# Two small products of the tensor engine rewritten, and the instruction order searched anew

## The chip, the core and the metric

The kernel runs on one core of a Trainium2 chip. A core has five engines with queues of their own: TensorE (PE, matmuls; PEld stands for its loads of weights), VectorE (DVE), ScalarE (ACT), GpSimd (POOL) and SyncE (SP, which issues most DMAs). The metric is the device time of one execution in microseconds, as the median of several runs: 402.71 us before the change, with single runs from 401.82 to 403.29.

## The reference

Two stages. The first is windowed attention over 8 batches, 8 heads, 576 positions and 64 channels; the second a gated attention of four experts on its output x.

```python
scores = scale * np.matmul(q, k.transpose(0, 1, 3, 2))      # stage 1, per batch and head
mask = (rel >= 0) & (rel < 64)                              # a window of 64 positions
attn = softmax(where(mask, scores, -1e9))
x = attn @ v                                                # heads side by side: 576 x 512
for e in range(4):                                          # stage 2, per batch
    q, k, v = x @ wq[e], x @ wk[e], x @ wv[e]               # 512 -> 64
    a = softmax(causal(scale * q @ k.T))
    out += gate[:, e] * (a @ v @ wo[e])                     # the best 2 of 4 experts by x @ w_gate
```

## The kernel before

Stage 1 works on pairs of heads: 32 pairs, 9 blocks of 64 queries each, in 72 groups. For a group `m` multiplies q and k (L344, fp32, tiles of 64 x 32 of the array), `q` is its softmax on DVE, ACT and POOL, `t` transposes (L414) and `a` multiplies with v (L440, tiles of 64 x 64) and writes x to SBUF as a high and a low fp16 part (L465 on ACT, L467 on DVE).

Before x is split in two fp16 parts it is scaled by a bound per batch: no entry of x is larger than the largest entry of v. Unit `n` (`s1_top`) reduces v of a batch to one maximum per partition, on DVE (L483, L486). Unit `M` (`s1_scale`) makes one number of these 128 and puts it on all partitions: a transpose by PE (L490), a maximum along the row by DVE (L493), a product of a row of ones with that number by PE (L495), and a scale and its reciprocal by DVE (L498, L499). Unit `N` works out further factors.

Stage 2 takes a batch b and a pair of experts pr at a time. `v`, `k` and `r` are the projections (L592 to L594, three fp16 products high x high, high x low, low x high, on the full array of 128 x 128). The projected q, transposed, has the 64 channels of one expert on partitions 0 to 63 and those of the other on 64 to 127. It is copied out of PSUM as a high part by ACT (L675) and a low one by DVE (L683; in batch 0 by POOL, L681) into `QT`; a projection is done in two halves of 320 and 256 queries. `x` multiplies q with k (L717, tiles of 64 x 128, one per expert), `y` is the softmax, `u` weighs it, `D` transposes it (by DMA, for the last pair partly by PE, L811), `A` multiplies with v (L843, tiles of 128 x 64), `o` is the output projection.

The first 64 queries of both experts are one unit `x` of their own, `k == 4`: six products of 64 x 64, three per expert, the one expert's result on partitions 0 to 63, the other's on 64 to 127 (L708).

The order of all work is written by hand in the table `ORDER`, a list of units: each name stands for the next step of that unit (up to its next `yield`), and the digits behind a colon name the PSUM banks that the step takes. Each engine runs its instructions in that order. Units `F` only keep PE busy: products of a constant matrix that nobody reads (L892); so do the first ones, whose number per bank is in `FILL` (L222).

Of the kernel before, what the change touches and what calls it, by code (L numbers as in the profile page):

```python
# [42 lines left out]
FILL = "44444444"  # L43

ORDER = (
# [101 lines left out]
)  # L147


@with_exitstack  # L150
def window_attention_moe_attention(ctx: ExitStack, tc: tile.TileContext, qT, kT, vW,
# [10 lines left out]
    def bank():  # L162
        return PS[:, banks.pop(0)]
# [844 lines left out]
```

## Time and profile before

| | |
|---|---|
| median of 3 runs | 402.71 us (401.82 to 403.29) |
| the profiled execution | 402.01 us |
| its span, first to last instruction | 400.3 us |
| mean granted clock of TensorE | 0.998 |
| PE busy | 385.6 us, 96% |
| DVE busy | 341.2 us, 85% |
| ACT busy | 330.9 us, 83% |
| POOL busy | 307.7 us, 77% |
| DMA, mean | 178 GB/s |

The rows quoted further down belong to this one profiled execution. A busy PE counts from the start of a matmul to its modelled end, and such records overlap; from one start to the next is what a matmul holds PE for. The idle time behind a bar in a row is the time in which the engine waited before it, with the one that ended it.

### The profile page before, as it was taken

Reading aid. Unit: us, or ns where it says so; the run is one execution under the profiler, and the core shown is the slowest. Engines: PE = TensorE matmul, PEld = TensorE weight load, DVE = VectorE, ACT = ScalarE, POOL = GpSimd, SP = SyncE. Lnnn points to the kernel's source line nnn. Section 1 sums busy time; section 2 is a strip of 40 time slices with the busy share of each in tenths; the row PEclk is TensorE's granted clock in tenths of the full one; section 3 lists DMA queues with packets and bytes.
Section 4 is the critical chain, followed back from the end, with each engine's and each line's share of the span. In section 5 each row is a group of like instructions: output and inputs, shape, how many; then the busy total and the mean of one; then the engine's idle time right before and its main releaser. Section 6 shows DMA issues by size and latency. Waiting matters only on the chain. (4 is left out here: it accounts for less than half of the span.)

```text
span 400.3 us, 18293 instructions
## 1 busy us (share of the span) xinstructions
PE 385.6 (96%) x7288; PEld 289.2 (72%) x7288; DVE 341.2 (85%) x1040; ACT 330.9 (83%) x1163; POOL 307.7 (77%) x686
## 2 busy tenths in 40 slices
PE   8899999999999999999999999999999999999985
PEld 8777777777777776777766866787767767777563
DVE  2898999899889778998898989888999698789872
ACT  2878899989788888898898998988989898876762
POOL 7375757988788888897698987898787986988520
PEclk9999999999999999999999999999999999999999
DMA  7942713699978987899959995799949592798993
GB/s 230 389 155 105 228 25 128 206 177 211 199 156 188 200 143 250 176 220 229 182 122 227 167 182 189 146 278 174 239 99 160 100 168 107 106 172 145 193 214 133
DMA packets 142677, 71.25 MB, mean 178 GB/s; under 512 B 123392, under 2 KB 126720, under 8 KB 142592
## 3 DMA queue, kind: packets, MB, share of 16 engines
q1 hardware_dynamic: 142080, 69.56, 80.1%
q8 instruction: 57, 0.93, 1.0%
q10 hardware_dynamic: 512, 0.52, 0.4%
q14 instruction: 28, 0.23, 0.2%
HBM read 30.94 MB, written 9.44 MB: 101 GB/s over the span
## 5 line engine op out<-in xcount | busy, mean ns | idle before, releaser
L794 POOL TENSOR_TENSOR sp<-p,sp 128x320 f16<-128x320 f32 (+3 forms) x110 | 101.6, 923 | 9.2
L732 ACT ACTIVATE p<-p,r 128x576 f32<-128x576 f32 (+3 forms) x128 | 77.5, 612 | 6.9 <-DVE r L728 5.9
L372 ACT ACTIVATE p<-ps,st 128x64 f32<-128x64 f32 x216 | 65.2, 320 | 10.0 <-POOL st L369 6.8
L783 ACT ACTIVATE sp<-p,r 128x320 f16<-128x320 f32 (+3 forms) x114 | 68.1, 615 | 2.7 <-POOL r L769 2.0
L793 POOL TENSOR_SCALAR p<-p,r 128x320 f32<-128x320 f32 (+3 forms) x110 | 65.0, 591 | 3.5 <-ACT sp L783 2.2
L728 DVE CUSTOM_DVE_ANT_0 p<-ps,causal,sc 128x320 f32<-128x320 f32 (+2 forms) x128 | 63.8, 541 | 4.4 <-PE ps L717 3.7
L397 POOL TENSOR_TENSOR p<-p,st 128x256 f32<-128x256 f32 x72 | 43.5, 613 | 6.4 <-DVE st L393 4.4
L418 DVE TENSOR_TENSOR pt<-ps,tri 128x1024 f32<-128x1024 f32 (+1 forms) x40 | 44.5, 1111 | 4.3 <-PE ps L414 3.2
L372 ACT ACTIVATION_READ_ACCUMULATOR p<-ps,st 128x1 f32 x216 | 45.8, 212 | 0.0
L717 PE MATMUL ps<-kt,qt 64*128 64x320 f16 (+3 forms) x480 | 40.1, 292 | 0.6 <-DVE r L728 0.3
L440 PE MATMUL ps<-pt,vt 64*64 64x128 f32 (+1 forms) x1440 | 39.3, 249 | 0.9 <-DVE xl L467 0.4
L440 PEld LDWEIGHTS ps<-pt,vt 64*64 64x64 f32 x1440 | 34.1, 133 | 8.2 <-DVE r L728 2.2
L843 PE MATMUL ps<-tu,v 128*64 128x64 f16 (+2 forms) x1056 | 39.0, 229 | 0.9 <-DMA tu<-sp 0.4
L843 PEld LDWEIGHTS <-v 128*64 128x64 f16 x1056 | 35.8, 111 | 4.6 <-issue 3.2
L344 PE MATMUL ps<-k,q 64*32 64x96 f32 (+2 forms) x2304 | 37.8, 244 | 0.8 <-issue 0.5
L592 PE MATMUL ps<-xh,wkhi 128*128 128x256 f16 (+1 forms) x128 | 36.7, 287 | 0.9 <-DVE p L379 0.5
L592 PE MATMUL ps<-xh,wqhi 128*128 128x320 f16 (+1 forms) x128 | 36.7, 287 | 0.1
L593 PE MATMUL ps<-xl,wqhi 128*128 128x320 f16 (+1 forms) x128 | 36.6, 286 | 0.0
L594 PE MATMUL ps<-xh,wklo 128*128 128x256 f16 (+1 forms) x128 | 36.6, 286 | 0.0
L594 PE MATMUL ps<-xh,wqlo 128*128 128x320 f16 (+1 forms) x128 | 36.6, 286 | 0.0
L593 PE MATMUL ps<-xl,wkhi 128*128 128x256 f16 (+1 forms) x128 | 36.6, 286 | 0.0
L344 PEld LDWEIGHTS ps<-k,q 64*32 64x32 f32 x2304 | 29.8, 106 | 9.3 <-issue 5.8
(168 smaller groups left out, 1022.7 us busy)
## 6 DMA issues: line engine op xcount, KB each, us to landing
vt<-in_vW_dram SPq DMA_DIRECT2D x16, 576.0 KB, 4.9
q<-in_qT_dram SPq DMA_DIRECT2D x14, 576.0 KB, 5.2
k<-in_kT_dram SPq DMA_DIRECT2D x14, 576.0 KB, 5.9
out_dram<-out SPq DMA_DIRECT2D x29, 256.0 KB, 3.2
tu<-sp SPq DMA_TRANSPOSE x94, 4.2
out_dram<-out SPq DMA_DIRECT2D x10, 128.0 KB, 3.7
q<-in_qT_dram SPq DMA_DIRECT2D x2, 320.0 KB, 7.8
k<-in_kT_dram SPq DMA_DIRECT2D x2, 320.0 KB, 8.1
```

The costliest lines, as they stand in the source:

```text
L344: nc.tensor.matmul(S1[g][o:o + 32, i, c:c + n], lhsT=q_t[r, i % 2, q0:q0 + 32], rhs=k_t[r, i % 2, k0:k0 + n], start=True, stop=True)
L372: nc.scalar.activation(pt[:, i], ps[:, i, 64:128], AF.Exp, bias=st[:, 0, z + i:z + i + 1], scale=0.125, accum_out=st[:, 1, z + i:z + i + 1])
L440: nc.tensor.matmul(to, lhsT=values[d][r, h, b + e - (w == 0)], rhs=rhs, start=(e, h) not in started, stop=s == n - 1, skip_group_check=True)
L592: nc.tensor.matmul(ps, lhsT=ah, rhs=bh, start=first, stop=False)
L593: nc.tensor.matmul(ps, lhsT=ah, rhs=bl, start=False, stop=False)
L594: nc.tensor.matmul(ps, lhsT=al, rhs=bh, start=False, stop=last)
L728: nc.vector.tensor_tensor_reduce(out=dst, in0=src, in1=mask, scale=SC[b][:, 3:4], scalar=above, op0=OP.add, op1=OP.min, accum_out=to)
L732: nc.scalar.activation(p, p, AF.Exp, bias=r2[:, 0, x:x + 1], scale=-1.0, accum_out=r2[:, 1, x:x + 1])
L783: nc.scalar.activation(hi, p, AF.Copy, scale=by)
L793: nc.gpsimd.tensor_scalar(p, p, by, 1.0, op0=OP.mult, op1=OP.mult)
L794: nc.gpsimd.tensor_tensor(lo, p, hi, op=OP.subtract)
L843: nc.tensor.matmul(to, lhsT=V2[b % 2][:, c, a, 2 * pr + h], rhs=rhs, start=n == 0, stop=n == len(work_list) - 1, skip_group_check=True)
```

## The change

The bound of v: POOL multiplies the 128 x 128 identity by the 128 maxima, which gives a diagonal matrix (now the last step of `s1_top`), and one product of a full matrix of ones with that diagonal puts all 128 maxima on every partition; DVE takes the maximum along the columns there. The first product, its bank and the 1 x 1 tile between are gone.

The first 64 queries: their projected q goes to a matrix `Q0` of 128 x 128, expert 0's block in the upper left, expert 1's in the lower right, zeros elsewhere (cleared once). One product on the full array then gives both experts' scores: three products of 128 x 128 by 64 columns in place of six of 64 x 64. To fill `Q0`, the copy of the first half of q becomes three copies, both for the high and the low part: one of 256 queries on all partitions, and two of 64 queries on half of them.

The table ORDER is another one throughout, and the fillers at the start are 5 per bank in place of 4, over the same 512 columns.

```diff
--- before.py
+++ after.py
@@ -40,110 +40,110 @@
-FILL = "44444444"
+FILL = "55555555"
 ORDER = (
-    'f:01234567 p0 p1 c l0 h0 h1 i l2 l1 z p0 Fa0_3:0 m2:7 p1 m0:6 l3 Fa1_4:5 m1:5 q0 h2 d q2 q0 e0 m3:4 q0 q1 w0 q1 '
...
+    'f:01234567 p0 c p1 l0 h0 h1 i l2 Fa0_3:0 m0:7 p0 z l1 p1 m2:6 q0 l3 Fa1_4:5 m3:5 q0 q2 h2 d m1:4 q0 q0 q0 q1 w0 '
...
@@ -203,7 +203,7 @@
     win = const.tile([128, 64], F32, name="win")
     tri = const.tile([128, 2, 64], F32, name="tri")
     above_one = const.tile([128, 128], BF16, name="above_one")
-    one = const.tile([1, 128], F32, name="one")
+    ones = const.tile([128, 128], F32, name="ones")
 
     past = win.bitcast(U32)
 
@@ -226,7 +226,7 @@
                                     channel_multiplier=1, compare_op=OP.is_ge, fill=NEG)
         make_identity(nc, ident)
         nc.gpsimd.memset(above_one, 1.015625)
-        nc.gpsimd.memset(one, 1.0)
+        nc.gpsimd.memset(ones, 1.0)
 
     def tri_constants():
         nc.vector.memset(tri, 1.0)
@@ -476,6 +476,7 @@
             nc.gpsimd.tensor_scalar(XT[b9 & ~1, x][:, :, b9 % 2], last, 1.0, 1.0, op0=OP.mult, op1=OP.mult)
 
     MV = {}
+    MD = {}
 
     def s1_top(b):
         MV[b] = work.tile([128, 3], F32, tag="mv", name=f"mv_{b}")
@@ -484,18 +485,20 @@
                                     axis=AX.X, op=OP.max, apply_absolute_value=True)
             yield
         nc.vector.tensor_tensor(MV[b][:, 2:3], MV[b][:, 0:1], MV[b][:, 1:2], op=OP.max)
+        yield
+        MD[b] = work.tile([128, 128], F32, tag="md", bufs=1, name=f"md_{b}")
+        nc.gpsimd.tensor_scalar(MD[b], ident, MV[b][:, 2:3], 1.0, op0=OP.mult, op1=OP.mult)
 
     def s1_scale(b):
-        ps = bank()
-        nc.tensor.transpose(ps[0:1, 0:128], MV[b][:, 2:3], ident)
-        yield
-        m = work.tile([1, 1], F32, tag="m1", name=f"m1_{b}")
-        nc.vector.tensor_reduce(m, ps[0:1, 0:128], axis=AX.X, op=OP.max)
-        yield
-        nc.tensor.matmul(ps[:, 256:257], lhsT=one, rhs=m, start=True, stop=True)
+
+        ps = bank()[:, 0:128]
+        nc.tensor.matmul(ps, lhsT=ones, rhs=MD[b], start=True, stop=True)
+        yield
+        m = MV[b][:, 0:1]
+        nc.vector.tensor_reduce(m, ps, axis=AX.X, op=OP.max)
         yield
         sc = SC[b] = work.tile([128, 5], F32, tag="sc", bufs=3, name=f"sc_{b}")
-        nc.vector.tensor_scalar(sc[:, 1:2], ps[:, 256:257], 1e-30, 1.0 / UP, op0=OP.max, op1=OP.mult)
+        nc.vector.tensor_scalar(sc[:, 1:2], m, 1e-30, 1.0 / UP, op0=OP.max, op1=OP.mult)
         nc.vector.reciprocal(sc[:, 0:1], sc[:, 1:2])
 
     def s2_scale(b):
@@ -511,6 +514,7 @@
 
     L = [const.tile([128, 5, E], F32, name=f"logits{i}") for i in range(2)]
     QT = [const.tile([128, 2, S], F16, name=f"qt{i}") for i in range(2)]
+    Q0 = [const.tile([128, 2, 2, 64], F16, name=f"q0_{i}") for i in range(2)]
 
     Y8 = [[const.tile([128, 2, 512], F16, name=f"y{b}{i}") for i in range(2)] for b in range(2)]
     Y1 = [const.tile([128, 2, 128], F16, name=f"y2{i}") for i in range(2)]
@@ -571,6 +575,8 @@
         nc.gpsimd.memset(below, 0.0)
         for e in range(1, E):
             nc.gpsimd.memset(below[:, e, 0:e], 1.0)
+        for x in Q0:
+            nc.gpsimd.memset(x, 0.0)
 
     def clear_v2(x):
         nc.gpsimd.memset(V2[x][64:128, 4], 0.0)
@@ -672,25 +678,35 @@
         return ps, c0, n
 
     def parts(b, x, ps, hi, lo):
-        nc.scalar.activation(hi, ps, AF.Copy, scale=1.0 / UP)
+
+        for r, c, to in hi:
+            nc.scalar.activation(to, ps[r, c], AF.Copy, scale=1.0 / UP)
         yield
         if b == 0:
             t = TURN[1][1][:, 320 * x:320 * x + ps.shape[-1]]
             nc.scalar.activation(t, ps, AF.Copy, scale=1.0 / UP)
             yield
-            nc.gpsimd.tensor_tensor(lo, t, hi, op=OP.subtract)
+            for (r, c, to), (_, _, up) in zip(lo, hi):
+                nc.gpsimd.tensor_tensor(to, t[r, c], up, op=OP.subtract)
         else:
-            nc.vector.scalar_tensor_tensor(lo, ps, 1.0 / UP, hi, op0=OP.mult, op1=OP.subtract)
+            for (r, c, to), (_, _, up) in zip(lo, hi):
+                nc.vector.scalar_tensor_tensor(to, ps[r, c], 1.0 / UP, up, op0=OP.mult, op1=OP.subtract)
 
     def s2_k(b, pr, half):
         ps, c0, n = proj(b, "k", pr, half)
         yield
-        yield from parts(b, half, ps, *(KT[pr][:, x, c0:c0 + n] for x in range(2)))
+        yield from parts(b, half, ps, *([(slice(0, 128), slice(0, n), KT[pr][:, x, c0:c0 + n])] for x in range(2)))
 
     def s2_q(b, pr, half):
         ps, c0, n = proj(b, "q", pr, half)
         yield
-        yield from parts(b, 2 + half, ps, *(QT[pr][:, x, c0:c0 + n] for x in range(2)))
+        if half:
+            to = [[(slice(0, 128), slice(0, n), QT[pr][:, x, c0:c0 + n])] for x in range(2)]
+        else:
+            to = [[(slice(0, 128), slice(64, n), QT[pr][:, x, 64:n])] +
+                  [(slice(64 * e, 64 * e + 64), slice(0, 64), Q0[pr][64 * e:64 * e + 64, x, e]) for e in range(2)]
+                  for x in range(2)]
+        yield from parts(b, 2 + half, ps, *to)
 
     SCORES = (((1, 0, 192), (2, 0, 320)), ((3, 0, 448),), ((4, 0, 320),), ((4, 320, 256),))
 
@@ -703,10 +719,8 @@
         if k == 4:
             ps = SB[b, pr, k] = bank()
             for x, (w, m) in enumerate(((0, 0), (0, 1), (1, 0))):
-                for e in range(2):
-                    r = slice(64 * e, 64 * e + 64)
-                    nc.tensor.matmul(ps[r, 0:64], lhsT=QT[pr][r, w, 0:64], rhs=KT[pr][r, m, 0:64],
-                                     start=x == 0, stop=x == 2)
+                nc.tensor.matmul(ps[:, 0:64], lhsT=Q0[pr][:, w].rearrange("r e q -> r (e q)"), rhs=KT[pr][:, m, 0:64],
+                                 start=x == 0, stop=x == 2)
             return
         ps = SB[b, pr, k] = [bank() for e in range(2)]
         for i, key, n in SCORES[k]:
```

On PE, the bound of v of batch 0 stood like this before. L490 is the transpose of the maxima (`mv`), L495 the product with ones, L414 transposes of stage 1, L344 scores of stage 1, L892 a filler:

```order
L344 MATMUL ps<-k_182,q_181 32x96 x4
L344 MATMUL ps<-k_178,q_177 32x96 x4
L344 MATMUL ps<-k_182,q_181 32x96 x4
L490 MATMUL ps<-ident,mv_347 1x128
L414 MATMUL ps<-ident,p_2_323 128x64 x4
L414 MATMUL ps<-ident,p_3_362 128x64 x4
L892 MATMUL ps<-ident 128x128 x3
L495 MATMUL ps<-m_0_478,one 128x1
L344 MATMUL ps<-k_178,q_177 32x96 x4
```

and stands like this now, where L906 is the filler and L495 the product of ones with the diagonal `md`:

```order
L344 MATMUL ps<-k_204,q_203 32x96 x4
L344 MATMUL ps<-k_188,q_187 32x96 x4
L344 MATMUL ps<-k_204,q_203 32x96 x4
L906 MATMUL ps<-ident 128x128
L495 MATMUL ps<-md_474,ones 128x128
L414 MATMUL ps<-ident,p_2_339 128x64 x4
L414 MATMUL ps<-ident,p_3_344 128x64 x4
L344 MATMUL ps<-k_188,q_187 32x96 x4
```

One instruction of PE is gone, and the one that is left stands behind a matmul of its own full shape.

On PE, the first 64 queries of batch 5 (`kt` and `qt` are the projected k and q, `pt` the weights of stage 1), before, with six such pairs of a load and a product in a row, of which three are shown:

```order
L440 MATMUL ps<-pt_46_4616,vt_85 64x128 x12
L440 MATMUL ps<-pt_46_4616,vt_85 64x64 x4
L708 LDWEIGHTS qt_106
L708 MATMUL ps<-kt_118,qt_106 64x64
L708 LDWEIGHTS qt_106
L708 MATMUL ps<-kt_118,qt_106 64x64
L708 LDWEIGHTS qt_106
L708 MATMUL ps<-kt_118,qt_106 64x64
```

and now, where `q_0` is the block diagonal, with three pairs in all and the output projection behind them:

```order
L440 MATMUL ps<-pt_46_4708,vt_85 64x128 x12
L440 MATMUL ps<-pt_46_4708,vt_85 64x64 x4
L722 LDWEIGHTS q_0_107
L722 MATMUL ps<-kt_119,q_0_107 128x64
L722 LDWEIGHTS q_0_107
L722 MATMUL ps<-kt_119,q_0_107 128x64
L722 LDWEIGHTS q_0_107
L722 MATMUL ps<-kt_119,q_0_107 128x64
L598 LDWEIGHTS y_111
```

Three pairs fewer; the results lie on the same 128 partitions.

On ACT, at the end of the loading stage, before (L268 and L286 work on the weights, L372 is the exponential of stage 1, L465 the first copies of x, `xh`):

```order
L286 ACTIVATE wqhi<-tu_83,factor 128x1024
L286 ACTIVATE wkhi<-tu_83,factor 128x1024
L268 ACTIVATE tu_81<-v_1_115 128x1024
L372 ACTIVATE p_4_475,st_4_474<-ps,st_4_474 128x64 x4
L372 ACTIVATE p_5_530,st_4_474<-ps,st_4_474 128x64 x4
L465 ACTIVATE xh_99<-ps,sc_527 128x4x128 x2
L286 ACTIVATE wohi<-v_1_115,factor 128x1024
```

and now:

```order
L286 ACTIVATE wqhi<-tu_83,factor 128x1024
L268 ACTIVATE tu_81<-v_1_117 128x1024
L372 ACTIVATE p_4_490,st_4_489<-ps,st_4_489 128x64 x2
L372 ACTIVATE p_5_493,st_4_489<-ps,st_4_489 128x64 x2
L372 ACTIVATE p_4_490,st_4_489<-ps,st_4_489 128x64 x2
L372 ACTIVATE p_5_493,st_4_489<-ps,st_4_489 128x64 x2
L465 ACTIVATE xh_99<-ps,sc_534 128x4x128
L372 ACTIVATE p_7_585,st_6_581<-ps,st_6_581 128x64 x4
L465 ACTIVATE xh_99<-ps,sc_534 128x4x128
L286 ACTIVATE wkhi<-tu_83,factor 128x1024
L286 ACTIVATE wohi<-v_1_117,factor 128x1024
```

The high part of wk moved from ahead of the first copies of x to behind the second.

## Rows read from the trace of the kernel before

**Rows 1.** The page's first part: busy time, share of the span, instructions.

```profile
PE 385.6 (96%) x7288; PEld 289.2 (72%) x7288; DVE 341.2 (85%) x1040; ACT 330.9 (83%) x1163; POOL 307.7 (77%) x686
```

**Rows 2.** Stretches: their length, busy time of each engine, PEclk, DMA, GB/s.

```profile
10.00:20.00 10.00, 8.22 (x107) 7.27 (x112) 8.60 (x23) 8.90 (x38) 3.28 (x8) 1.00 1.04 389
...
60.00:100.00 40.00, 38.61 (x769) 29.84 (x773) 36.96 (x115) 36.91 (x139) 34.06 (x82) 1.00 0.87 181
...
200.00:250.00 50.00, 48.81 (x949) 35.36 (x944) 46.27 (x140) 45.02 (x160) 41.78 (x91) 1.00 0.83 177
...
22.00:372.00 350.00, 344.96 (x6682) 257.37 (x6681) 310.93 (x952) 302.64 (x1084) 287.73 (x626) 1.00 0.81 171
```

**Rows 3.** Waits of PE: who waited for whom, us, times, longest.

```profile
PE ps L490 <- DVE mv L486: 1.2, 2, 0.6
```

**Rows 4.** Timeline of PE: start, us, instruction; a q projection, v, a score.

```profile
220.11 0.30 PE L594 MATMUL ps<-xh,wqlo 128*128 128x320 f16 x1
...
221.35 0.27 PE L593 MATMUL ps<-wvlo,xh 128*128 128x260 f16 x1
221.46 0.27 PE L594 MATMUL ps<-wvhi,xl 128*128 128x260 f16 x1
221.67 0.56 PE L717 MATMUL ps<-kt,qt 64*128 64x192 f16 x8
```

**Rows 5.** Timeline of PE at the transpose, the first queries, fillers, the row product.

```profile
21.07 0.27 PE L490 MATMUL ps<-ident,mv 128*1 128x128 f32 x1 [0.54 <-DVE mv L486]
21.28 0.46 PE L414 MATMUL ps<-ident,p 64*128 64x64 f32 x8
...
58.64 0.38 PE L708 MATMUL ps<-kt,qt 64*64 64x64 f16 x12
58.95 0.71 PE L892 MATMUL ps<-ident 128*128 128x128 f32 x4
59.49 0.27 PE L490 MATMUL ps<-ident,mv 128*1 128x128 f32 x1
...
101.81 0.38 PE L495 MATMUL ps<-m,one 1*128 1x1 f32 x2
102.12 0.58 PE L717 MATMUL ps<-kt,qt 64*128 64x320 f16 x6
```

**Rows 6.** Groups by line and shape: count, busy us, mean ns, idle before.

```profile
L592 PEld LDWEIGHTS <-wqhi 128*128 128x128 f16 x128 | 12.5, 98 | 4.7 <-issue 1.1
...
L793 POOL TENSOR_SCALAR p<-p,r 128x192 f32<-128x192 f32 x26 | 11.0, 425 | 1.0 <-ACT sp L783 0.8
...
L675 ACT ACTIVATE qt<-ps 128x320 f16<-128x320 f32 x16 | 7.1, 442 | 2.0 <-PE ps L594 2.0
...
L683 DVE SCALAR_TENSOR_TENSOR qt<-ps,qt 128x320 f16<-128x320 f32 x14 | 6.7, 481 | 1.1 <-ACT qt L675 1.0
...
L675 ACT ACTIVATE qt<-ps 128x256 f16<-128x256 f32 x16 | 6.1, 379 | 1.7 <-PE ps L594 1.6
L683 DVE SCALAR_TENSOR_TENSOR qt<-ps,qt 128x256 f16<-128x256 f32 x14 | 5.8, 416 | 1.1 <-ACT qt L675 1.1
...
L849 ACT ACTIVATE y<-ps 128x64 f16<-128x64 f32 x16 | 3.6, 224 | 0.0
...
L852 DVE SCALAR_TENSOR_TENSOR y<-ps,y 128x64 f16<-128x64 f32 x16 | 3.3, 211 | 0.0
...
L708 PEld LDWEIGHTS <-qt 64*64 64x64 f16 x96 | 3.0, 107 | 1.5 <-issue 0.9
```

**Rows 7.** Timeline of PE: transposes of the last pair.

```profile
384.12 1.15 PE L811 MATMUL ps<-ident_h,sp 128*128 128x128 f16 x14 [0.40 <-DVE sp L781]
```

**Rows 8.** Timeline of DVE: the low part of q ahead of 221.67.

```profile
220.91 0.49 DVE L683 SCALAR_TENSOR_TENSOR qt<-ps,qt 128x320 f16<-128x320 f32 x1
```

**Rows 9.** Timeline of ACT: the split of wk, the first copy of x.

```profile
19.90 1.23 ACT L286 ACTIVATE wkhi<-tu,factor 128x1024 f16<-128x1024 f32 x1
...
26.36 0.69 ACT L465 ACTIVATE xh<-ps,sc 128x512 f16<-128x512 f32 x1 [0.49 <-PE ps L440]
```

200 rows, old and new, of the table ORDER are left out of this document.

## Prediction

> **What bounds the kernel now.** I read the page's busy shares first, then the stretches of time, then TensorE's (PE's) waits and its rows in order of time. PE is busy 385.6 us, 96% of the span, the next engine, VectorE (DVE), 341.2 [rows 1]. The table by stretches says the same by stage: from 22 to 372 us PE is busy 344.96 of 350 us, so no more than 5.0 us are idle there, while DVE has 39 and ScalarE (ACT) 47 us to spare. In the loading stage PE is short of work (8.22 of 10 us from 10 to 20) [rows 2]. So time is won by making PE's stream shorter, and lost where PE is made to wait. The waits of PE are small and scattered: the largest on a line of this change is the transpose in the bound of v waiting for DVE, 1.2 us in two places [rows 3].
>
> A busy PE here says little of what one matmul costs, because records overlap; I use the distance from one start to the next. Two neighbours of one array shape that stream 260 columns start 0.11 us apart (221.35, 221.46), but the last one before a change of shape is followed after 0.21 us (221.46, 221.67). So a change of array shape costs about 0.1 us [rows 4]. Counting neighbours of unlike shape in the two orders of PE gives 266 before and 249 after. If the matmuls of the bound of v are left out of both lists, 249 and 249 remain: all 17 that go belong to that part.
>
> **The change part by part.** All sums are against the profiled execution, 402.01 us (span 400.3 and 1.7 around it). The median of the three runs, 402.71, is 0.7 above it; I add that at the end.
>
> 1. The bound of v, 8 times. Removed: a transpose (L490) and a product of one row (L495). The product takes 0.31 us to the next start (101.81, 102.12), the transpose 0.21 (21.07, 21.28) [rows 5], both with the change of shape behind them: 8 x (0.31 + 0.21) = 4.1 us. Added: one full fp32 product of 128 columns. The filler L892 is that very operation: two of them, 58.95 to 59.49, take 0.54 with the shape changed once behind them, so (0.54 - 0.1) / 2 = 0.22 each [rows 5]. In 7 of 8 places the new product stands behind a matmul of its own shape, as in the first order shown, so no change of shape is added: 8 x 0.22 = 1.8. Gain 2.3 us; with 0.27 each, if the change of shape behind it counted, 1.9.
>
> 2. What the same part makes PE wait for. Before, PE waited twice for DVE; the chain then went PE, DVE, PE, DVE. After, GpSimd (POOL) scales the 128 x 128 identity, and PE waits for that. No row shows 128 columns; the same operation takes 425 ns on 192 [rows 6], so at most 8 x 0.43 = 3.4 us on an engine that is busy 77% [rows 1]. Behind it on POOL stand normalisations that DVE and PE come to later. If the two exposed waits grow by that whole step it is 2 x 0.43 = 0.9 us, if the saved round trip repays it 0: I take 0.5 lost. The reduce and the two small steps on DVE stay, one for one.
>
> 3. The first 64 queries, 16 units in 14 places (two stand together twice). Before: twelve products of a quarter array take 0.31 us to the next start (58.64, 58.95) [rows 5]; less 0.1 that is 18 ns each, 96 x 0.018 = 1.7 us. Both forms cause the same number of changes of shape (8 with all else left as it is). After: 48 full products of 64 columns. The lower bound is the 18 ns again, 48 x 0.018 = 0.9; the upper one is a full product of 128 columns with a load of its own each time, the transposes at the end: 14 in 1.15 us, 0.082 each, 3.9 us [rows 7]. I take 0.035, nearer to the row with the same 64 columns: 1.7, a gain of 0, between -2.2 and +0.8.
>
> The load of the weights decides within these ends. Before, 64 columns took 107 ns; the loads of 128 columns of the projections take 98 [rows 6]. So the wider load is not dearer in the row. The Trainium skill, page "TensorE: Matmul & The Clock Gate", section "LDWEIGHTS (loading the stationary operand)", says the opposite: the time goes with the columns, P / 1.2 ns, 107 for 128 and 53 for 64, which would make the block diagonal the slower form. The rows here don't show that doubling. It is rival C.
>
> 4. The evacuation of the first half of q, 16 times. One ACT pass over 320 columns (442 ns) becomes one over 256 (379) and two over 64 on half the partitions; the row nearest to these is the copy of y, 64 columns, 224 ns [rows 6]. 16 x (379 + 2 x 224 - 442) = 6.2 us more on ACT. On DVE 14 x (416 + 2 x 211 - 481) = 5.0 us more (the first batch does this on POOL) [rows 6]. Both lie beside PE: 47 and 39 us are free. A tight place of before shows the cover: the last product of a q projection starts at 220.11 [rows 4], DVE is done with its low part at 221.40 [rows 8], and the score starts at 221.67, straight behind the v products and their change of shape [rows 4]. Cost 0 while such work stands between; if it didn't, up to 16 x (385 + 357) ns = 11.9 us.
>
> 5. The new order. Loading: ACT's split of wk (1.23 us at 19.90) stood ahead of the first copy of x (26.36); now it stands behind two of them, as the third order shows [rows 9]. Before that copy ACT waited 0.49 for PE [rows 9], so ACT was not last there, and the gain lies between 0 and 1.2; I take 0.5. The loads of the first pair's second half move ahead of wk's weights, which are needed later too: 0. Fillers behind 27 us fall from 7 to 3; at 0.22 each that is 0.9, but they stood where PE had to wait: 0 to 0.9, taken 0.4. At the end one product of weights and values (unit A701) goes from ahead of the last transposes to behind them: PE has the same sum of work, taken as 0.
>
> Sum: 2.3 - 0.5 + 0 + 0.5 + 0.4 = 2.7 us. 402.01 - 2.7 = 399.3 profiled, and with 0.7, 400.0 for the median of the runs.
>
> **Rivals.**
> A. PE's freed time comes back as waits, and the time stays, about 402.7. For it: every buffer and bank was placed anew, ACT and DVE carry 11.2 us more, and 2.7 us is half of what PE idles in the middle. Against: the work removed was on PE itself, with nothing behind it.
>
> B. Slower: DVE becomes the bound in the stretches where it is fullest, 36.96 of 40 us from 60 to 100 and 46.27 of 50 from 200 to 250 [rows 2]. Its place is the first half of q between projection and score. Of the 11.9 us, more than 4.7 (2.7 gained and 2.0 to show) would have to be uncovered, that is 40%; with half it is 5.9 - 2.7 = 3.2 slower, 405.9. For it: between 221.40 and 221.67 the margin is 0.27 us [rows 4, 8]. Against: ACT's and DVE's free time, and only the whole chain counts, not each pass.
>
> C. The wider weight load decides: 48 x 0.098 = 4.7 us for the block diagonal, 3.0 more than the 1.7 before. Then 400.0 + 3.0 = 403.0. Rows 6 and 7 speak against it.
>
> **How the numbers follow.** Forecast 0.57, A 0.24, B 0.12, C 0.07. A measurement of this kernel tells about 0.5%, 2.0 us, from no change, so faster means under 400.7. The forecast's own range, with the bounds of parts 1 to 5, is 397.5 to 402.0; a fifth of it lies above 400.7, but the unknown placing of waits can also help by 1 or 2 us in A and C. Faster 0.56, same 0.32, slower 0.12. The range that holds 8 in 10 reaches from 396.8 to 403.8.
>
> **What would show it.** Right: 249 changes of shape and a PE busy time lower by 2 to 3 us; the product of ones about 0.22 to the next start; the block diagonal about 0.1 us for three; PE's idle time between 22 and 370 us still near 5; ACT up by about 6 and DVE by about 5 us. Wrong: the product of ones waiting for POOL by more than half a us in several places; scores waiting for the copies of q (A if little, B if over 5 us); three products of the diagonal taking 0.3 us (C); or an end whose chain after the last transposes is longer by over 1 us.

## The result and the profile after

| | before | after |
|---|---|---|
| median, 10 executions each | 402.88 us (401.08 to 403.50) | 405.02 us (403.23 to 406.72) |
| the profiled execution | 402.01 us | 406.72 us |
| its span | 400.3 us | 403.7 us |

The ratio is 1.0055, with a 95% interval of 1.0034 to 1.0076: 2.1 us slower, where 400.0 was forecast and 403.8 was the upper end of the range. The profiled execution of after is the slowest of its ten. In the mean of these ten, 2.35 us of the time lie outside the span, against 1.73 us in the 112 executions of before that the runs below were compared with; so some 0.6 us of the loss lie there, and no run shows why. One of a_olddiag's twelve executions below took 2042.2 us, is slow and is in no ratio; without it the median of that run is 401.76.

The page's busy line of after, which answers to [rows 1]:

```profile
PE 384.8 (95%) x7233; PEld 289.0 (72%) x7234; DVE 349.4 (87%) x1068; ACT 335.0 (83%) x1195; POOL 311.3 (77%) x700
```

Three of the stretches of [rows 2], with the columns of that group:

```profile
60.00:100.00 40.00, 37.61 (x738) 28.41 (x738) 37.53 (x118) 35.67 (x140) 33.20 (x87) 0.96 0.81 185
200.00:250.00 50.00, 49.77 (x985) 37.48 (x982) 46.33 (x148) 45.90 (x170) 41.23 (x94) 1.00 0.92 184
22.00:372.00 350.00, 340.74 (x6582) 254.45 (x6585) 315.56 (x968) 305.21 (x1109) 287.50 (x632) 1.00 0.78 169
```

From 22 to 372 us PE is busy 340.74 us, against 344.96 before: its idle time went from 5.0 to 9.3 us. That doesn't make PE's stream 4.2 us shorter, since what isn't done by 372 us is done behind it. Over the whole span PE is busy 384.8 us in place of 385.6 [rows 1], and idle 18.9 us in place of 14.7. So the later end is in waits.

Four waits of PE in after, which answer to [rows 3]:

```profile
PE ps L414 <- DVE wvlo L291: 1.7, 1, 1.7
PE ps L495 <- POOL md L490: 1.5, 1, 1.5
PE ps L722 <- DVE kt L693: 1.0, 1, 1.0
PE ps L598 <- DVE kt L693: 1.0, 1, 1.0
```

The first is in the loading stage. The second is the product of ones waiting for the diagonal; the other two are PE waiting for DVE's low part of the projected k. L693 is the line on which DVE makes the low parts of k and of q, and it is where the change added work. The pieces of the change by group, which answer to [rows 6] (line, engine, operation, shapes, count, busy us, mean ns, idle before):

```profile
L693 DVE SCALAR_TENSOR_TENSOR qt<-ps,qt 128x256 f16<-128x256 f32 x28 | 11.5, 413 | 1.5 <-ACT qt L683 1.1
L693 DVE SCALAR_TENSOR_TENSOR q<-ps,q 64x64 f16<-64x64 f32 x28 | 6.0, 216 | 0.2
L683 ACT ACTIVATE q<-ps 64x64 f16<-64x64 f32 x32 | 6.9, 215 | 0.2
L490 POOL TENSOR_SCALAR md<-ident,mv 128x128 f32<-128x128 f32 x8 | 3.0, 374 | 0.5 <-DVE mv L487 0.4
L722 PEld LDWEIGHTS <-q 128*128 128x128 f16 x48 | 2.4, 97 | 2.6 <-issue 1.3
```

The three products of the block diagonal hold PE for 0.10 us together (148.80 to 148.90), where a product of the same array shape follows; where another shape follows, for 0.18 to 0.19 us unless k is late:

```profile
148.80 0.26 PE L722 MATMUL ps<-kt,q 128*128 128x64 f16 x3
148.90 0.38 PE L598 MATMUL ps<-wohi,y 128*128 128x512 f16 x1
```

### The profile page after: what moved, and what is told of

Same layout as the page of the kernel before. It is cut to its first block, busy times and chain, and to the rows that moved or that the text cites. A ratio compares the mean times of both kernels' runs of the same rounds, so it can differ in the third digit from the quotient of the medians.

```text
span 403.7 us, 18292 instructions
## 1 busy us (share of the span) xinstructions
PE 384.8 (95%) x7233; PEld 289.0 (72%) x7234; DVE 349.4 (87%) x1068; ACT 335.0 (83%) x1195; POOL 311.3 (77%) x700
## 4 chain that ended last, share of the span: by engine, by line
PE 55%; DVE 21%; POOL 8%; ACT 6%; issue 5%; DMA 4%; SPq 1%; DVEq 0%; POOLq 0%; ACTq 0%
PE ps L598 9%; PE ps L600 9%; PE ps L599 8%; PE ps L731 7%; PE ps L857 6%; PE ps L440 6%; PE ps L344 6%; POOL sp L808 3%; DVE p L742 3%; DVE sp L801 2%; POOL p L807 2%; DMA tu<-in_wk_dram 2%; PE ps L414 2%; DVE pt L418 2%; DMA tu<-in_wv_dram 2%
## 5 line engine op out<-in xcount | busy, mean ns | idle before, releaser
L372 ACT ACTIVATE p<-ps,st 128x64 f32<-128x64 f32 x216 | 65.1, 319 | 14.1 <-POOL st L369 13.5
L797 ACT ACTIVATE sp<-p,r 128x576 f16<-128x576 f32 (+3 forms) x114 | 68.6, 619 | 3.7 <-POOL r L783 3.5
L397 POOL TENSOR_TENSOR p<-p,st 128x256 f32<-128x256 f32 x72 | 44.6, 627 | 12.1 <-DVE st L393 8.4
L372 ACT ACTIVATION_READ_ACCUMULATOR p<-ps,st 128x1 f32 x216 | 45.9, 213 | 0.0
L731 PE MATMUL ps<-kt,qt 64*128 64x320 f16 (+3 forms) x480 | 42.0, 297 | 1.0 <-DVE qt L693 0.2
L344 PE MATMUL ps<-k,q 64*32 64x96 f32 (+2 forms) x2304 | 38.5, 247 | 0.9 <-DVE mv L498 0.3
L598 PE MATMUL ps<-xh,wqhi 128*128 128x256 f16 (+1 forms) x128 | 36.7, 287 | 0.0
L599 PE MATMUL ps<-xl,wqhi 128*128 128x256 f16 (+1 forms) x128 | 36.6, 286 | 0.0
L600 PE MATMUL ps<-xh,wqlo 128*128 128x256 f16 (+1 forms) x128 | 36.6, 286 | 0.0
L344 PEld LDWEIGHTS ps<-k,q 64*32 64x32 f32 x2304 | 30.2, 107 | 8.2 <-issue 2.4
```

The lines of the kernel that those rows point to most:

```text
L344: nc.tensor.matmul(S1[g][o:o + 32, i, c:c + n], lhsT=q_t[r, i % 2, q0:q0 + 32], rhs=k_t[r, i % 2, k0:k0 + n], start=True, stop=True)
L372: nc.scalar.activation(pt[:, i], ps[:, i, 64:128], AF.Exp, bias=st[:, 0, z + i:z + i + 1], scale=0.125, accum_out=st[:, 1, z + i:z + i + 1])
L598: nc.tensor.matmul(ps, lhsT=ah, rhs=bh, start=first, stop=False)
L599: nc.tensor.matmul(ps, lhsT=ah, rhs=bl, start=False, stop=False)
L600: nc.tensor.matmul(ps, lhsT=al, rhs=bh, start=False, stop=last)
L731: nc.tensor.matmul(ps[e][:, at(i):at(i) + n], lhsT=QT[pr][r, w, q], rhs=KT[pr][r, m, key:key + n], start=x == 0, stop=x == 2)
```

## The experiments

Every time is the median of one kernel, every ratio is to executions of before on the same chip, with its 95% interval. The table has the runs that differ in order and forms; the others follow in the text, by question.

| run | order of | bound of v | first queries | median us | ratio to before |
|---|---|---|---|---|---|
| after | after | new | new | 405.02 | 1.0055 (1.0034 to 1.0076) |
| b_bound | before | new | old | 406.14 | 1.0083 (1.0056 to 1.0110) |
| b_diag | before | old | new | 407.47 | 1.0114 (1.0078 to 1.0150) |
| b_both | before | new | new | 410.64 | 1.0187 (1.0150 to 1.0224) |
| a_olddiag | after | new | old | 402.02 | 0.9974 (0.9949 to 0.9999) |
| a_none | after | old | old | 407.15 | 1.0110 (1.0082 to 1.0139) |

**The parts apart.** I began with a theory that the new order was the loser and the two new forms were sound (theory O). Rivals: waits for POOL's diagonal (M), and the three copies of q (Q).

b_bound is the order of before and, of the diff, only the new `s1_top` and `s1_scale`. In the order, POOL's step stands right behind the maximum, and the product of ones where the transpose stood:

```diff
-... n0 ... n0 ... n0 ...
+... n0 ... n0 ... n0 n0 ...
```

> The order of before, the new bound of v in it (POOL's multiplication right behind the maximum), the old six products of the first queries. Theory O (the new order is what costs; the new forms save as predicted): 2.3 less PE work, 0.5 or less given back as a wait for POOL, so about 401 us, 0.995 of before (402.9). Theory M (the product of ones waiting for POOL is what costs): no faster than before, 403 to 404.5, with waits of L495 for POOL over 1 us in the trace. Theory Q (the block diagonal costs): like O here.

Measured: 406.14. Theory O falls, and M's 403 to 404.5 is too low as well, though its sign is there: PE waits 2.1 us for POOL, in two places (the line stands with b_free below).

b_diag is the order of before with the old bound and, of the diff, `Q0`, `parts`, `s2_q` and the products of `k == 4`.

> The order of before, the old bound, the block diagonal alone. Theory O: the same as before within 0.8 us, 402 to 403.5, since the three products take what six took. Theory Q (three copies of q in place of one make scores wait): over 404 us, the most of the 2.1 us that after lost or more. Theory M: like O here.

Measured: 407.47, far over 404. The block diagonal alone costs 4.6 us in the order of before.

b_both is the two together, in the order of before.

> The order of before with both new forms: after without its new order. Theory O: about 401 us, 0.995 of before, 4 us under after (405.0). Theories M and Q, and any theory by which the forms cost: 404 us or more, near after. The granted clock stays at 1.00 throughout by O.

Measured: 410.64, about the sum of the two losses (3.3 and 4.6, by the ratios). The new order is what makes after 5 us better than this.

a_olddiag is after with the old first queries; `parts`, `s2_q` and the products are those of before, of which the products are shown:

```diff
-                nc.tensor.matmul(ps[:, 0:64], lhsT=Q0[pr][:, w].rearrange("r e q -> r (e q)"), rhs=KT[pr][:, m, 0:64], ...)
+                for e in range(2):
+                    r = slice(64 * e, 64 * e + 64)
+                    nc.tensor.matmul(ps[r, 0:64], lhsT=QT[pr][r, w, 0:64], rhs=KT[pr][r, m, 0:64], ...)
```

> After with its new order and new bound, but the old six products of 64 x 64 and the old single copies of q. Theory O: the same as after, 405 within 1 us. Theory Q: back to 403 or lower. Theory M: the same as after.

Measured: 402.02, ratio 0.9974. With the block diagonal gone, the loss is gone. So theory Q holds as to the cost, if not yet as to its way: by the ratios the block diagonal costs 0.0081 x 402.9 = 3.3 us in the new order, all that after lost and more. Whether this version beats before is at the edge of what the runs show: the interval ends at 0.9999, and that of a repeat (c_load below) at 1.0001.

**Which half of the block diagonal.** The change has PE's three full products on one side, ACT's and DVE's three copies in place of one on the other. Two runs cross them.

a_nocopy takes the copies away:

```diff
     def s2_q(b, pr, half):
-        if half:
+        if True:
```

> After, with the three full products of the block diagonal kept, but q evacuated by the old single copies; the block diagonal stays at zeros, so the scores of the first 64 queries are left out of what is computed. PE's new form without ACT's and DVE's extra copies. Theory B (the copies of q on ACT and DVE are what the block diagonal costs): 402 us, within 1 of the version with the old form (402.0). Theory C (PE's wide products are): 405, as after.

a_copies takes the full products away:

```diff
-                nc.tensor.matmul(ps[:, 0:64], lhsT=Q0[pr][:, w].rearrange("r e q -> r (e q)"), ...)
+                for e in range(2):
+                    nc.tensor.matmul(ps[r, 0:64], lhsT=Q0[pr][r, w, e], rhs=KT[pr][r, m, 0:64], ...)
```

> After, with the three copies of q into the two blocks kept, but read by the old six products of 64 x 64, one block each. PE's old form with ACT's and DVE's extra copies. Theory B: 405 us within 1, as after. Theory C: 402 within 1.

Measured: a_nocopy 401.23, ratio 0.9959 (0.9934 to 0.9984); a_copies 404.55, ratio 1.0052 (1.0026 to 1.0078). The time goes with the copies, whichever products read them. That the full products gain anything by themselves is not shown: a_nocopy is 0.6 us below a_olddiag by the ratios, and the intervals overlap.

**Whose copies.** a_act leaves DVE's two small copies out, a_dve ACT's:

```diff
+            to[1] = to[1][:1]                                               # a_act
+            to[0] = [(slice(0, 128), slice(0, n), QT[pr][:, 0, 0:n])]       # a_dve
```

> After, with ACT's three copies of the high part of q, but on DVE one pass over 256 columns; the low part of the first 64 queries is left out. If the copies that stand on DVE's queue are the cost (theory D): 402 us within 1. If those on ACT's queue are (theory A): 405 within 1. If both share it: between, 403 to 404.

> After, with DVE's three copies of the low part of q, but on ACT one pass over all 320 columns; the high part of the first 64 queries is left out of the block diagonal. Theory D: 405 us within 1. Theory A: 402 within 1. Shared: between.

Measured: a_act 402.75, ratio 0.9991 (0.9973 to 1.0009); a_dve 403.49, ratio 1.0007 (0.9986 to 1.0028). Both lie between a_nocopy and after, and their intervals overlap with each other but not with after's: each engine's copies cost something, DVE's 2.6 us and ACT's 1.9 us by the ratios as read from after, and which costs more isn't settled.

**How the copies reach PE.** The alignment of equal PE instructions in a_olddiag and after shows the largest single loss in the middle at 184 us, 0.82 us in one step. DVE there in a_olddiag, and PE's next projection:

```profile
182.52 0.48 DVE L686 SCALAR_TENSOR_TENSOR qt<-ps,qt 128x320 f16<-128x320 f32 x1
182.93 0.41 DVE L367 TENSOR_REDUCE st<-ps 128x4 f32<-128x256 f32 x1
183.26 0.47 DVE L686 SCALAR_TENSOR_TENSOR kt<-ps,kt 128x320 f16<-128x320 f32 x1
```

```profile
183.38 0.27 PE L597 MATMUL ps<-xh,wklo 128*128 128x256 f16 x1
183.78 0.30 PE L595 MATMUL ps<-xh,wkhi 128*128 128x320 f16 x1
```

The same place in after:

```profile
185.61 0.41 DVE L693 SCALAR_TENSOR_TENSOR qt<-ps,qt 128x256 f16<-128x256 f32 x1
185.94 0.45 DVE L693 SCALAR_TENSOR_TENSOR q<-ps,q 64x64 f16<-64x64 f32 x2
186.42 0.42 DVE L367 TENSOR_REDUCE st<-ps 128x4 f32<-128x256 f32 x1
186.87 0.49 DVE L693 SCALAR_TENSOR_TENSOR kt<-ps,kt 128x320 f16<-128x320 f32 x1
```

```profile
186.19 0.27 PE L600 MATMUL ps<-xh,wklo 128*128 128x256 f16 x1
187.42 0.30 PE L598 MATMUL ps<-xh,wkhi 128*128 128x320 f16 x1 [0.95 <-DVE kt L693]
```

The two small copies stand on DVE's queue between the first pass over q and the low part of k. PE's next projection takes the bank that this pass over k frees. In a_olddiag the pass starts 0.12 us before PE's last product (183.26, 183.38), and PE is held for 0.3 us (0.40 from start to start, where 0.11 is usual); in after it starts 0.68 us behind it (186.87, 186.19), and PE waits 0.95. No score waits for q here: a projection waits for k. With the copies left out (a_nocopy) the same two products start 0.41 us apart, and in after 1.23, so this place is worth 0.82 us.

The other wait for k in after's list is at 359 us, where a product of the first queries needs the low part of k and DVE's copies of q are ahead of it. In after, and then in a_nocopy:

```profile
359.27 0.22 PE L722 MATMUL ps<-kt,q 128*128 128x64 f16 x2 [0.99 <-DVE kt L693]
```

```profile
355.47 0.22 PE L722 MATMUL ps<-kt,q 128*128 128x64 f16 x2 [0.48 <-DVE kt L693]
```

Both waits go with DVE's copies. In a_dve, which keeps them, they are as long as in after:

```profile
PE ps L725 <- DVE kt L695: 1.0, 1, 1.0
PE ps L598 <- DVE kt L695: 1.0, 1, 1.0
```

and in a_act, which leaves them out, they are not:

```profile
PE ps L723 <- DVE kt L693: 0.4, 1, 0.4
PE ps L598 <- DVE kt L693: 0.2, 1, 0.2
```

So the way by the low part of k is shown for about 0.8 + 0.5 = 1.3 us of the 3.3 to 3.9. The rest comes in smaller steps that no run takes apart, and how ACT's copies reach PE isn't shown.

a_qpool keeps the block diagonal and lets POOL fill it:

```diff
+        if not half:
+            for e in range(2):
+                r = slice(64 * e, 64 * e + 64)
+                nc.gpsimd.tensor_copy(Q0[pr][r, :, e], QT[pr][r, :, 0:64])
```

> After, with q evacuated by the old single copies, and the block diagonal filled from there by POOL, two copies of 64 partitions per half of q (high and low part together), behind DVE's low part. If only the load on ACT and DVE costs: 401.2 to 402, as with the copies left out. If the score of the first 64 queries or POOL's own queue is late by the step more: 403 or above.

Measured: 412.27, ratio 1.0232 (1.0201 to 1.0264), 11 us over a_nocopy. The 32 copies are 9.5 us on POOL, and POOL is idle before them for DVE:

```profile
L711 POOL COPY q<-qt 64x128 f16<-64x128 f16 x32 | 9.5, 297 | 4.9 <-DVE qt L693 3.7 <-DVE st L393 0.2
```

POOL is busy 78% in a_olddiag, and yet 9.5 us more in its queue make the kernel longer by more than that. How much of it is the copies' time, and how much what POOL waits for ahead of them, the run doesn't separate.

a_late moves the small copies to a step of their own, later in the order:

```diff
+        yield from parts(b, 2, ps, *(x[:1] for x in to))
+        yield
+        yield from parts(b, 2, ps, *(x[1:] for x in to))
```

> After, with the two small copies of q on ACT and the two on DVE moved to a later place in the order in batches 1 to 7, as late as the bank of the projection and the score that reads them allow (4 to 58 steps later); the same work, another place in the queues. If the place is what costs (they stand ahead of work that PE waits for): 403 us or lower. If it is their work on two full engines, wherever it stands: 404.5 to 405.5.

Measured: 414.14, ratio 1.0317 (1.0271 to 1.0362). Neither expectation. Waits of PE there:

```profile
PE ps L600 <- DVE q L695: 4.0, 4, 1.7
PE ps L729 <- DVE q L695: 3.0, 2, 2.1
PE ps L738 <- DVE q L695: 2.0, 2, 1.3
```

These are 9.0 us together, about what a_late takes more than after. The copies read the bank of q's projection, so a late copy holds that bank against its next user, and the product of the first queries (L729) waits for the copy itself. At 186 us the wait of 0.95 is gone, and at 194 PE waits 0.82 for the moved copy:

```profile
194.28 0.27 PE L600 MATMUL ps<-xh,wkhi 128*128 128x256 f16 x1 [0.82 <-DVE q L695]
```

Place does count, but the run doesn't show that a better place exists; whether the copies could be hidden in another order is open.

**The bound of v.** c_m1 is a_olddiag with the product of ones of batch 1 behind a product of stage 1:

```diff
-'M1:0 q18 q17 q17 a10:34 M1 q18 g00 M1 q17 g00 q16 u000 t14 q18 ...
+'q18 q17 q17 a10:34 q18 M1:0 g00 q17 g00 M1 q16 u000 t14 M1 q18 ...
```

> The new order with the new bound and the old first queries, and in batch 1 the product of ones moved behind the product of weights and values (a10), so that PE has 0.9 us of work while POOL makes the diagonal. Theory W (the 1.5 us that PE waits for POOL there reaches the end): about 1 us less than without the move, 401. Theory S (PE is held up there by DVE anyway, and the wait moves on to another line): the same, 402 within 0.5.

Measured: 402.42, ratio 1.0004 (0.9984 to 1.0024); no gain. PE at that place in a_olddiag, and in c_m1:

```profile
61.40 0.49 PE L495 MATMUL ps<-md,ones 128*128 128x128 f32 x2 [1.48 <-POOL md L490]
61.81 1.00 PE L440 MATMUL ps<-pt,vt 64*64 64x128 f32 x32
```

```profile
61.11 1.00 PE L440 MATMUL ps<-pt,vt 64*64 64x128 f32 x32 [1.74 <-DVE r L731]
62.04 0.49 PE L495 MATMUL ps<-md,ones 128*128 128x128 f32 x2
62.46 0.87 PE L720 MATMUL ps<-kt,qt 64*128 64x448 f16 x7
64.11 0.56 PE L720 MATMUL ps<-kt,qt 64*128 64x320 f16 x5 [0.78 <-DVE sc L501]
```

The wait went to the line that is now first, and that line waits for DVE (L731), not for the diagonal. In a_olddiag, too, POOL itself is kept waiting: DVE's maximum (L487) ends at 60.86 us and POOL's step starts at 60.97, after an idle 0.37. The move has a price of its own: a score now waits 0.78 us, put down to the scale (L501) that comes behind the product. So theory S fits, but the run doesn't show what the wait for POOL would cost by itself.

a_none is the new order with both old forms. The old bound has one step more, and its bank is taken again early in five batches, so its product and scaling had to be put ahead of that, as in batch 0:

```diff
-M0 t3 q5 q4 m6:26 w2 M0
+M0 t3 M0 q5 q4 M0 m6:26 w2
```

> The new order with both old forms: the old bound's product and its scaling put where the bank allows, the old first queries. If the new bound gains what PE saves (2.3 us): 404 to 405, 2 to 3 above the version with the new bound alone (402.0). If the new bound costs here as it does in the order of before (3.2 us there): 399 to 400.

Measured: 407.15, by the ratios 5.5 us above a_olddiag. So the new order with the old bound, as I placed it, is much slower. PE waits there 1.1 us for the row maximum (L494) and 1.0 us for L487, so part of this is my placing; that the new bound gains in the new order is likely, but how much isn't shown.

b_free is b_bound without the wait:

```diff
-        nc.tensor.matmul(ps, lhsT=ones, rhs=MD[b], start=True, stop=True)
+        nc.tensor.matmul(ps, lhsT=ones, rhs=ident, start=True, stop=True)
```

> The order of before with the new bound alone, but the product of ones reads the constant identity, so it waits for nothing but its bank; POOL still makes the diagonal. The bound's value is left out of what is computed. Theory M (in that order the waits for POOL's diagonal are what made the new bound dearer, 406.1): 401 to 402. If it is the place of the other steps or the loading stage: 404 to 406.

Measured: 404.49, ratio 1.0031 (1.0011 to 1.0051). Of the 3.3 us that the new bound costs in the order of before, the waits for POOL are 2.1 by the ratios, which is also what the first of these lines of b_bound's trace has:

```profile
PE ps L495 <- POOL md L490: 2.1, 2, 1.1
PE ps L414 <- POOL p L397: 1.7, 5, 0.5
```

Of the other 1.2 us, and of the 2.3 us of PE's saving that went in that order, a part stands on another line: PE waits 1.7 us for POOL's normalisations in b_bound and in b_free as well, against 0.4 us in before. POOL makes the diagonal in both, so this fits the step in POOL's queue; no run leaves out that step alone.

**The loading stage.** c_load was to move DVE's first reduce of v (L484) behind the reciprocal that POOL's first normalisation waits for. No engine's order changed by the edit, so it is a repeat of a_olddiag on another chip. c_load2 makes the move:

```diff
-'q3 q1 n0 w0 q1 q2 q1 w0 ...
+'q3 q1 w0 q1 q2 q1 n0 w0 ...
```

> The new order with the new bound and the old first queries (402.0), and in the loading stage DVE's first reduce of v moved behind the reciprocal that POOL's first normalisation waits for, so that PE's 1.7 us before its first transposes gets shorter. If that wait reaches the end: 401 us or lower. If the loading stage is bound by what comes after it: the same, 402 within 0.5.

> The new order with the new bound and the old first queries (0.9974 of before), and now DVE's reciprocal really ahead of its first reduce of v, so that POOL's first normalisation no longer runs beside DVE's low part of wv, and PE's 1.7 us before its first transposes gets shorter. If that wait reaches the end: 0.995 of before or lower. If the loading stage is bound by what comes after it: 0.997 as without the edit.

Measured: c_load 401.04, ratio 0.9974 (0.9948 to 1.0001); c_load2 401.05, ratio 0.9970 (0.9944 to 0.9997). PE in c_load2:

```profile
14.57 0.68 PE L414 MATMUL ps<-ident,p 64*128 64x64 f32 x8
16.48 0.60 PE L273 MATMUL ps<-tu,above_one 128*128 128x256 bf16 x4 [1.23 <-ACT tu L268]
...
19.14 0.60 PE L273 MATMUL ps<-tu,above_one 128*128 128x256 bf16 x4 [1.39 <-ACT tu L268]
```

The transposes come without their wait of 1.7 us, which a_olddiag and after have alike (the first line of after's waits), and two later products then wait 1.23 and 1.39 us for ACT. PE is held there by ACT's passes over the weights, and the edit gives back what it won.

## Why the prediction was wrong

**The step that failed is part 4, the evacuation of q.** It put 6.2 us on ACT and 5.0 us on DVE, which is what they are: 32 x 0.215 us - 16 x (442 - 383) ns = 5.9 us, and 28 x 0.216 us - 14 x (481 - 413) ns = 5.1 us. It then took them at nothing because "47 and 39 us are free". The runs show 3.3 us (after against a_olddiag) to 3.9 us (after against a_nocopy) in its place. Two mistakes made it. The free time was a sum over 350 us, while what counts is how far DVE is ahead of PE at each place; and the place that I looked at was the score that reads q. The work behind the copies on the same queue was not named: the low part of k, whose bank PE's next projection takes. That way is shown for 1.3 us of the loss; by which waits the rest of it reaches PE stays open.

**Rival B** had the mechanism, but the wrong place: "the first half of q between projection and score". Its point of decision, 4.7 of 11.9 us, was not reached by the copies alone. After is slower because less of the rest arrived than it and the forecast took for granted. That its 405.9 lies near the 405.0 measured is partly luck: it had 5.9 us lost and 2.7 gained, the runs 3.3 and 1.0.

**Parts 1 and 2, the bound.** PE's saving is there: 249 changes of array shape in place of 266, and in a_olddiag, over the whole span, a busy time of 381.9 us in place of 385.6, fewer fillers among it. After's own profile has 384.8, not the 2 to 3 us less that were named as a sign; two stretches at 1.2 GHz are in it (one is shown below, the other lies between 18 and 22 us), while a_olddiag's granted clock is 1.00 up to 398 us. The product of ones takes 0.32 us to the next start in five of its eight places in after and up to 0.42 in the others, a change of shape included; less 0.1 that is the 0.22 of the forecast or a little more. The wait for POOL was taken at 0.5 and bounded by 0.9 us; it is 1.5 in one place alone, so the bound was wrong, since it counted POOL's step and not DVE's queue ahead of it. In the order of before the waits cost 2.1 us (b_free). In the new order moving one of them away gained nothing (c_m1).

**Part 3, PE's products of the block diagonal**, held: 0.10 us for three, as the list of signs had it. Rival C falls: the loads take 97 ns for 128 columns, and a_copies, with six small products, is no faster than after beyond the intervals.

**Part 5, the new order.** Without the block diagonal, the forecast's terms sum to 2.7 us of gain (2.3 - 0.5 + 0.5 + 0.4); a_olddiag shows 1.0 (0.0 to 2.1 by the interval). The loading stage gives nothing that c_load2 could bring back. From 22 to 372 us a_olddiag's PE is idle 7.6 us against 5.0 before, so 2.6 us of the shorter stream came back as waits there, which is rival A (over the whole span PE is busy 3.7 us less and idle 2.7 us more):

```profile
22.00:372.00 350.00, 342.36 (x6656) 254.70 (x6656) 312.80 (x955) 303.86 (x1088) 291.49 (x633) 1.00 0.80 171
```

One more sign of being wrong came, a longer end behind the last transposes. Before they end at 385.84 of 400.3 us, in after at 386.72 of 403.7, so the end takes 17.0 us in place of 14.5. It takes 17.0 in a_olddiag too, so it belongs to the order and not to the copies. 36 products of weights and values more stand there, and PE waits twice in after:

```profile
387.88 0.94 PE L857 MATMUL ps<-tu,v 128*64 128x256 f16 x29 [0.94 <-DVE tu L167]
392.70 2.87 PE L857 MATMUL ps<-tu,v 128*64 128x256 f16 x72 [0.58 <-DVE out L891]
```

Ahead of the transposes the wait of before [rows 7] is gone, so only a part of the 2.5 us is lost; how much, no run takes apart.

The forecast's own range was too narrow by its own bounds: with 1.9 gained in part 1, 0.9 lost in part 2 and 2.2 in part 3 its upper end is 403.9, not 402.0, and the 11.9 us of part 4 are not in it.

So the 2.1 us slower are 1.0 gained by bound and order, and 3.3 lost by the copies, each known to about 1 us.

## What to carry to other kernels

An engine that is 15% idle over the whole can still be the one that its neighbour waits for: before calling added work hidden, go through what stands behind it on its own queue, up to the next bank or tile that the bounding engine takes. A form that saves on the bounding engine by giving two others more instructions should be timed alone, with the products and the copies crossed, and both in the order that is kept: in the order of another form each of the two forms here cost 3 to 5 us. A wait that the profile names is worth only what is not late anyway behind it, as c_load2 shows.

## What was not expected of the hardware

**Small DVE operations are held by POOL.** L643 works on 128 x 4 or 128 x 16 values of two tiles in SBUF; its 12 executions in after take from 164 to 1129 ns:

```profile
L643 DVE TENSOR_TENSOR gt<-gt,half x12: 164/516/1129, 63.1 to 360.5; 128x16 f32<-128x16 f32 x8, 128x4 f32<-128x4 f32 x4
```

One of them beside what POOL does at that time:

```profile
184.13 0.95 DVE L643 TENSOR_TENSOR gt<-gt,half 128x4 f32<-128x4 f32 x1
```

```profile
184.03 1.03 POOL L808 TENSOR_TENSOR sp<-p,sp 128x448 f16<-128x448 f32 x1
```

It ends 0.02 us behind POOL's operation (185.08, 185.06). So do all seven of the twelve that take over 0.4 us: each began while an operation of POOL was running and ends 0.01 to 0.03 us behind it. The Trainium skill, page "SBUF — State Buffer", section "Who interferes with whom", says that a DVE instruction with two inputs in SBUF and a GpSimd instruction that reads SBUF exclude each other for the whole instruction; the trace agrees. The other direction is in the loading stage: two normalisations of POOL (L397) take 2.11 us beside DVE's low part of wv in a_olddiag, and 1.18 us in c_load2, where they run beside a reduce with one input.

```profile
15.79 2.11 POOL L397 TENSOR_TENSOR p<-p,st 128x256 f32<-128x256 f32 x2 [1.45 <-DVE st L393]
```

```profile
13.67 1.18 POOL L397 TENSOR_TENSOR p<-p,st 128x256 f32<-128x256 f32 x2
```

Whether such locks are part of why one order suits one form only wasn't tried.

**TensorE's clock** fell to 1.2 GHz for a few us in after's profile, after PE had been nearly idle:

```profile
60.00:62.00 2.00, 0.62 (x11) 0.43 (x10) 1.97 (x9) 2.00 (x11) 1.47 (x5) 1.00 0.54 100
...
64.00:66.00 2.00, 2.00 (x12) 0.57 (x8) 1.89 (x4) 1.60 (x9) 1.61 (x7) 0.50 0.38 145
```

In a_olddiag PE was as idle there (0.60 of 2.00 us), and the clock stayed at 1.00 from 62 to 66. It doesn't explain the result. Among executions with a mean granted clock of 0.996 or more, after takes 404.3 us in the mean of 4 and before 402.0 in the mean of 43; among those below, 405.7 (6) and 403.6 (69). The small gain of a_olddiag does depend on it: with its repeat c_load it takes 402.0 us (10 executions) at 0.996 or more, as before does, and 401.7 (13) below. So a gain of that version is seen only where before's clock is the lower one.
